# Five of eight slices of the split w1 and w2 are formed beside phase two's first pair, and stores move to GpSimd's queue

## The chip, the cores and the metric

The kernel runs on one core of one Trainium2 chip. The metric is the device time of one launch in microseconds (us). The time of a version is the median of several runs. A profiled execution also gives its span, from the first instruction to the last.

## The reference, cut to what matters

The inputs are float32 in the reference's code, and the ten arrays come to the kernel as 64-bit floats, which it reads as pairs of 32-bit words. Chunked attention (8 batches, 8 heads, 576 positions, chunks of 64) gives x of 4608 tokens by 512. Two gated products follow.

```
attn = softmax(scale * q_c @ k_c^T)          # in chunks of 64
x    = (attn @ v_c)  as [4608, 512]
x    = ((x @ w_a) * (x @ w_b)) @ w_out       # d_ff 1536: phase 0 below
out  = ((x @ w1) * (x @ w2)) @ w3 @ w_out2   # d_ff 1024: phase 1 below
```

## The kernel before, in words

The text calls the phase with d_ff 1536 phase one (`ph == 0` in the code) and the one with d_ff 1024 phase two (`ph == 1`). Tokens are worked in nine blocks of 512. Every matrix operand is split into a high and a low float32r part, and each product takes three passes (`SEQ`) of 128x512 matmuls.

Blocks are taken in pairs by a Strassen scheme of seven products (`strassen_step`) in place of eight. It works on slices of 128 columns of d_ff: twelve slices in phase one, eight in phase two. Its operands for each slice are the split pair of weights and two sums of them, four weight tiles. Block 0 and 1 go through plain products while weights are still being converted, pairs 1 to 3 of phase one through the scheme, and block 8 alone (the lone stage) through plain products again. Phase two has four pairs and block 8 alone.

The second product of a pair's first block follows slice by slice (`Second.part`). That of its second block comes afterwards in one stretch, which the code calls a burst. Its operands gh and gl are made by `ready` on ScalarE and GpSimd. After the last slice each 128x512 accumulator is copied out (`ev`, L845) and stored (L848) to a scratch in DRAM (`x2d`, 36 stores) or to the output (36 stores). Both kinds were issued by ScalarE's queue.

Weights are converted from 64-bit by `Conv`, driven by `Pump`. `float32_job` converts one piece of w3, w_out2, w1 or w2 and stores it as float32 in DRAM (40 stores, ScalarE's queue). A conversion's load goes to a slot of SBUF that an earlier conversion's store must have left.

In the lone stage `between` builds phase two's operands, while block 8 goes through twelve plain steps: 16 conversions of w1 and w2, w3 turned on TensorE (`turn_w3`), w3 @ w_out2 fused (`fuse`), and for each of the eight slices `Sums`: load the float32 pair, form two sums (`add`), split own parts (`own`) and sums (`early`), store all four tiles. These pieces are to be spent over 45 of the stage's 60 points, which is nine of its twelve steps.

A `Track` spreads pieces over points of a step. At one point it emits at most one piece that needs TensorE. SyncE's queue issues nearly all loads, in program order. Loads of q, k and v are put on a list (`ask`). `tick(loads=n)` issues n of them, and `settle` issues all that a unit needs at once. In phase one's pairs each of the seven products of a step ticks with 2 and each of the four parts of the second product with 1.

Of the kernel before, what the change touches and what calls it, by code (L numbers as in the profile page):

```python
# [18 lines left out]
NT = 512  # L19
# [59 lines left out]
def chunk_attention_two_gated_products(  # L79
# [55 lines left out]
    def store(to, src, wait=2, queue=None):  # L135

        stores.append([2 - wait, queue or nc.scalar, to, src])
# [490 lines left out]
    def w_tile(n, name):  # L628
        return pool.tile([P, 2, 2, 2, P], F32R, tag=f"w{n}", name=name)
# [4 lines left out]
    def by_part(t, s):  # L634

        return t[:, :, s].rearrange("p o k n -> p o (k n)")
# [32 lines left out]
    def float32_job(conv, to):  # L669


        def sink(w):
            store(to, w, 5)
            return (lambda: None), (lambda: None)

        return (conv, sink, nc.gpsimd)
# [48 lines left out]
    class Sums:  # L725
# [29 lines left out]
            split(by_part(t, 0), by_part(t, 1), v2, nc.vector)  # L755
            store(dw[self.ph][self.f][2 + i], whole(t).bitcast(F32), 2, nc.gpsimd)

        def own(self, m):


            o = slice(m, 2)
            t = w_tile(2 + m, f"w{self.ph}_{self.f}_o{m}")
            v2 = self.w[:, m].rearrange("p (o n) -> p o n", o=2)
            split(by_part(t, 0)[:, o], by_part(t, 1)[:, o], v2[:, o], nc.vector)
            store(dw[self.ph][self.f][m][:, m * NT :], whole(t)[:, m * NT :].bitcast(F32))

        def early(self, i):
            t = w_tile(6 + i, f"w{self.ph}_{self.f}_s{i}")
# [31 lines left out]
                n += 1  # L800

    def product(ps, w, x, begins):
        tick(loads=2)
        n = 0
        for wp, xp in SEQ:
            for kt in range(2):
                nc.tensor.matmul(  # L807
                    ps,
                    w[:, wp, kt],
                    x[:, kt, xp],  # L810
                    start=(begins and n == 0),
                    stop=(n == 5),
                    skip_group_check=True,
                )
                n += 1

    class Second:
# [6 lines left out]
        def part(self):  # L824
            m, ph, f, w, g = self.m, self.ph, self.f, self.w, self.g
            if m == 4:
                return
            self.m += 1
            tick(loads=1)
            acc = self.sums  # L830
            if f == 0:
                acc.append(psum.tile([P, NT], F32, tag=self.tags[m], name=f"acc{ph}_{self.j}_{m}"))
            ms = slice(m * P, (m + 1) * P)
            for wp, gp in SEQ:
                a, b = (w[:, wp, ms], g[gp]) if ph == 0 else (g[gp][:, ms], w[:, wp])
                nc.tensor.matmul(  # L836
                    acc[m],
                    a,
                    b,
                    start=(f == 0 and (wp, gp) == SEQ[0]),  # L840
                    stop=(f == NF[ph] - 1 and (wp, gp) == SEQ[-1]),
                )
            if f == NF[ph] - 1:
                t = pool.tile([P, NT], F32, tag="ev", name=f"ev{ph}_{self.j}_{m}", bufs=4)
                nc.scalar.copy(t, acc[m])  # L845
                j = self.j
                to = x2d[j][m] if ph == 0 else out[j * NT + m * P : j * NT + (m + 1) * P, :]
                nc.scalar.dma_start(to, t)  # L848

        def rest(self):  # L850
            while self.m < 4:
# [219 lines left out]
    with tc.manual_schedule():  # L1071
# [101 lines left out]
                pump.load(slot(6), nc.scalar)  # L1173
            tick(loads=8)
        units = unit_list(1)
        late = Track(attention_pieces(U[NHP:]), 5 * AHEAD)
        at = None
        for n, (T, f) in enumerate(order):
            if T == 0:
                conv = Track([conv_piece()] * (1 if f == 0 else 3), 5 if f + 1 < AHEAD else 8)  # L1180
                if f + 1 == NF[0]:
                    conv = None
            if T == 1 and f == 0:
                late.finish()
                attention_begins(units)
                at = Track(attention_pieces(units), 4 * (len(order) - n) - 2)

            def point(pe=True):
                if conv:
                    conv.point(pe)  # L1190
                (at or late).point(pe)

            if n + 1 == len(order):
                state["ready"] = ready(0, 1, 0, plain[0])
            plain_step(0, 0, T, f, f"0_{T}_{f}", point, plain[0], sums[0], "AC")
            if conv and (T == 1 or f + 1 < AHEAD):
                conv.finish()
                pump.flush()
# [11 lines left out]
        def summed(ph, f, n):  # L1210
            tag = dict(tag=f"Y{n % 3}")
            return Sums(ph, f, tag)

        def block_steps(ph, sb, x, at):

            single = sb == NSB
            j = LONE if single else 2 * sb
            nm = f"{ph}{sb}"
            new = ph == 0 and sb == 1
            sums, gplaces = [], None if single else []  # L1220
            n = NF[ph]
            su = first_sums
            last = single
            for f in range(n):
                extra = None
                if new:
                    if f + 2 < n:
                        su[f + 2] = summed(ph, f + 2, f + 2)
                        su[f + 2].load()
                    extra = Track(su[f + 1].pieces() if f + 1 < n else [], 5)  # L1230

                def freed(i):
                    if f + 2 < n:
                        if not new or i in (0, 3):
                            load_part(ph, f + 2, i)
                    elif ph == 0 and sb + 1 == NSB:
                        if i < 2:
                            load_plain(ph, f + 2 - n, i)
                    elif not last:
                        load_part(ph, f + 2 - n, i)  # L1240

                def point(pe=True):
                    if extra:
                        extra.point()
                    for a in at:
                        a.point(pe)

                if f + 1 == n and not single:
                    state["ready"] = ready(ph, j + 1, 0, gplaces)
                wo = state["outs"].next()  # L1250
                strassen_step(ph, j, f, x, f"{nm}_{f}", point, gplaces, sums, wo, freed)
                if extra:
                    extra.finish()
            for a in at:
                a.finish()
            return j, gplaces
# [20 lines left out]
        def between(got):  # L1277


            w3s, sums = [], []  # L1280
            turns = [(i, c) for i in range(NF[1]) for c in range(2)]
            for n_, ic in enumerate(turns + [None] * 2):
                if n_ >= 2 and n_ % 2 == 0:
                    w3s.append((1.5, True, lambda i=n_ // 2 - 1: fuse(i)))
                if ic:
                    w3s.append((1.0, True, lambda ic=ic: turn_w3(*ic)))
            su = [Sums(1, f, dict(tag=f"xo{3 + f % 2}")) for f in range(NF[1])]
            sums += [(0.1, False, su[0].load), (0.1, False, su[1].load)]
            for f in range(NF[1]):
                sums += su[f].early_pieces()  # L1290
                if f + 2 < NF[1]:
                    sums.append((0.1, False, su[f + 2].load))
            pump.cap = len(pump.jobs)
            pump.load(slot("L"))
            pump.load(slot("L"))
            conv = later_conv(2 * NF[1], "L")
            return merged((0, 1, w3s), (0, 0.75, conv), (0.3, 1, sums), (0, 0.5, x2_pieces([0, 1], got)))

        PTS = 7
        first_sums = {}  # L1300
# [3 lines left out]
        for ph, sb in [(0, sb) for sb in range(1, NSB + 1)] + [(1, sb) for sb in range(NSB + 1)]:  # L1304
# [5 lines left out]
            if lone:  # L1310
                x, pieces = lone_pieces(x32, f"{ph}{sb}")
                pieces = pieces + o2_pieces()
            elif not begins:
                x, pieces = strassen_pieces(x32, f"{ph}{sb}", sb == NSB)
            if ph == 0 and sb == 1:
                for f in range(2):
                    first_sums[f] = summed(ph, f, f)
                    first_sums[f].load()
                for f in range(2):
                    for i in (0, 3):  # L1320
                        load_part(ph, f, i)
                pieces = pieces + first_sums[0].pieces()
            steps, at, conv = NF[ph], [], []
            if ph == 0 and not lone:
                units = unit_list(sb + 1)
                attention_begins(units)
                work = attention_pieces(units)
                n_pts = PTS * steps + steps - 4
                if sb == NSB - 1:
                    pump.cap += 3 * NF[1]  # L1330
                    pump.load(slot(3))
                    pump.load(slot(3))
                    conv = later_conv(3 * NF[1], 3)
                    work = merged((0, 1, work), (0, 1, conv))
                    n_pts = PTS * steps
                at.append(Track(work, n_pts - 3))
# [92 lines left out]
```

## Time and profile before

| | |
|---|---|
| median of 3 runs | 1714.83 us (1713.59 to 1719.84) |
| the profiled execution | 1716.43 us, of which its span is 1714.6 us |
| TensorE (PE) busy | 1583.5 us, 92% of the span |
| VectorE (DVE), ScalarE (ACT), GpSimd (POOL) busy | 897.8, 552.3, 506.8 us |
| mean granted TensorE clock | 0.973 of full speed |
| moved by DMA | 409.56 MB, a mean of 239 GB/s |

The span is read by stages, since the engines and the queues have different limits in each. Block 0 and 1 take the time up to about 323 us with their burst. The pairs of phase one run to 955 us, with bursts at about 504, 710 and 922 us. The lone stage runs from 955 to 1145 us, and phase two fills the rest. Its first pair's steps run from 1145 to 1245 us.

### The profile page before, as it was taken

Reading aid. Unit: us, or ns where it says so; the run is one execution under the profiler, and the core shown is the slowest. Engines: PE = TensorE matmul, PEld = TensorE weight load, DVE = VectorE, ACT = ScalarE, POOL = GpSimd, SP = SyncE. Lnnn points to the kernel's source line nnn. Section 1 sums busy time; section 2 is a strip of 40 time slices with the busy share of each in tenths; the row PEclk is TensorE's granted clock in tenths of the full one; section 3 lists DMA queues with packets and bytes.
Section 4 is the critical chain, followed back from the end, with each engine's and each line's share of the span. In section 5 each row is a group of like instructions: output and inputs, shape, how many; then the busy total and the mean of one; then the engine's idle time right before and its main releaser. Section 6 shows DMA issues by size and latency. Waiting matters only on the chain.

```text
span 1714.6 us, 24613 instructions
## 1 busy us (share of the span) xinstructions
PE 1583.5 (92%) x8968; PEld 1265.1 (74%) x8968; DVE 897.8 (52%) x1460; ACT 552.3 (32%) x989; POOL 506.8 (30%) x450
## 2 busy tenths in 40 slices
PE   4779998899998999898999788899999999999998
PEld 3558786677776877676777676688878878878787
DVE  5767773766756555646786266552252252342331
ACT  4434443322243222322324223332141241242232
POOL 1434552222233111423335122212231232232322
PEclk9889999999999999999999899899999999999999
DMA  8667775877867887788987799987676676665684
GB/s 217 215 189 224 259 237 174 229 231 226 251 214 210 215 227 208 203 254 270 300 310 249 241 325 370 343 312 230 216 227 219 211 236 215 212 226 196 222 277 164
DMA packets 300536, 409.56 MB, mean 239 GB/s; under 512 B 176000, under 2 KB 196480, under 8 KB 300416
## 3 DMA queue, kind: packets, MB, share of 16 engines
q1 hardware_dynamic: 265568, 318.85, 61.4%
q0 software_dynamic: 12864, 46.14, 6.9%
q10 hardware_dynamic: 21984, 43.00, 6.7%
q8 instruction: 71, 1.16, 0.3%
q14 instruction: 49, 0.40, 0.1%
HBM read 321.91 MB, written 85.98 MB: 238 GB/s over the span
## 4 chain that ended last, share of the span: by engine, by line
PE 61%; DMA 13%; issue 8%; DVE 8%; POOL 4%; ACT 3%; SPq 2%; ACTq 0%; POOLq 0%; DVEq 0%
PE P L807 36%; PE acc L836 18%; SPq L148 2%; DMA wo<-dwo 2%; DMA d<-cv 2%; DMA cv<-in_moe_w_dram 2%; PE wf L1060 2%; PE pa L793 1%; DMA qk<-in_q_dram 1%; DVE c L895 1%; DMA cv_w<-in_moe_w_dram 1%; DMA dw<-w_o 1%; PE x L396 1%; PE pb L793 1%; DMA su<-d 1%
## 5 line engine op out<-in xcount | busy, mean ns | idle before, releaser
L807 PE MATMUL P<-xP,w 128*128 128x512 f32 (+1 forms) x3192 | 739.7, 385 | 25.0 <-DVE c L895 17.8
L807 PEld LDWEIGHTS P<-xP,w 128*128 128x128 f32 x3192 | 576.5, 189 | 157.9 <-DVE c L895 25.2
L895 DVE TENSOR_TENSOR c<-P,c 128x512 f32<-128x512 f32 (+1 forms) x228 | 150.0, 661 | 342.6 <-PE P L807 333.9
L923 POOL TENSOR_TENSOR G<-c,c 128x512 f32<-128x512 f32 x68 | 88.8, 1306 | 382.5 <-DVE c L895 382.3
L892 ACT COPY c<-P 128x512 f32<-128x512 f32 (+1 forms) x228 | 128.5, 564 | 223.3 <-PE P L807 219.7
L242 ACT CAST gh<-c 128x512 fp32r<-128x512 f32 x68 | 42.2, 621 | 356.6 <-DVE c L922 351.1
L243 POOL TENSOR_TENSOR gl<-c,gh 128x512 fp32r<-128x512 f32 x68 | 90.5, 1330 | 179.9 <-ACT gh L242 177.7
L836 PE MATMUL acc<-gh,wo 128*128 128x512 f32 x384 | 141.1, 405 | 0.0
L922 DVE TENSOR_TENSOR c<-P,c 128x512 f32<-128x512 f32 x68 | 46.9, 690 | 135.5 <-PE P L807 135.4
L836 PE MATMUL acc<-wo,gh 128*128 128x512 f32 x320 | 111.3, 391 | 0.5 <-ACT gh L242 0.5
L836 PEld LDWEIGHTS acc<-gh,wo 128*128 128x128 f32 x384 | 73.7, 192 | 16.8
L195 POOL TENSOR_TENSOR cv<-cv 128x512 f32<-128x512 f32 x40 | 46.8, 1170 | 107.7 <-DVE cv L189 76.4
L793 PE MATMUL pa<-xq,w 128*128 128x512 f32 x288 | 77.4, 421 | 0.0
L836 PE MATMUL acc<-gl,wo 128*128 128x512 f32 x192 | 76.5, 399 | 0.0
L793 PE MATMUL pb<-xq,w 128*128 128x512 f32 x288 | 71.9, 400 | 0.0
L845 ACT COPY ev<-acc 128x512 f32<-128x512 f32 x72 | 42.3, 588 | 88.8 <-PE acc L836 79.0
L836 PEld LDWEIGHTS acc<-wo,gh 128*128 128x128 f32 x320 | 60.1, 188 | 14.0 <-ACT gh L242 1.0
L243 DVE TENSOR_TENSOR xP<-xP,xP 128x512 fp32r<-128x512 f32 (+1 forms) x56 | 48.4, 905 | 40.5 <-ACT xP L242 40.5
L793 PEld LDWEIGHTS pa<-xq,w 128*128 128x128 f32 x288 | 57.5, 204 | 13.3
L836 PE MATMUL acc<-wo,gl 128*128 128x512 f32 x160 | 63.1, 394 | 0.8 <-POOL gl L243 0.8
L793 PEld LDWEIGHTS pb<-xq,w 128*128 128x128 f32 x288 | 54.5, 192 | 11.5
L1060 PE MATMUL wf<-wo,w3t 128*128 128x512 f32 x192 | 51.6, 429 | 11.6 <-DVE w3t L243 11.6
(153 smaller groups left out, 2358.8 us busy)
## 6 DMA issues: line engine op xcount, KB each, us to landing
w<-dw SPq DMA_DIRECT2D x228, 512.0 KB, 4.5
wo<-dwo SPq DMA_DIRECT2D x168, 512.0 KB, 4.6
dw<-w POOLq DMA_DIRECT2D x48, 512.0 KB, 5.1
w<-dw SPq DMA_DIRECT2D x92, 256.0 KB, 3.4
su<-d SPq DMA_DIRECT2D x20, 512.0 KB, 5.8
cv_o<-in_moe_w_out_dram SPq DMA_DIRECT2D x18, 512.0 KB, 5.4
x2d<-ev ACTq DMA_DIRECT2D x36, 256.0 KB, 4.8
x<-x2d SPq DMA_DIRECT2D x36, 256.0 KB, 4.7
```

The lines of the kernel that those rows point to most:

```text
L195: eng.tensor_tensor(self.w, hi.bitcast(F32), lo, op=ALU.add)
L242: nc.scalar.copy(dst_h, src)
L243: eng_l.tensor_tensor(dst_l, src, dst_h, op=ALU.subtract)
L793: nc.tensor.matmul(ps, w[m][:, kk // 2, wp, kk % 2], xq[kk // 2][:, kk % 2, xp], start=(n == 0), stop=(n == 3 * KM - 1),)
L807: nc.tensor.matmul(ps, w[:, wp, kt], x[:, kt, xp], start=(begins and n == 0), stop=(n == 5), skip_group_check=True,)
L836: nc.tensor.matmul(acc[m], a, b, start=(f == 0 and (wp, gp) == SEQ[0]), stop=(f == NF[ph] - 1 and (wp, gp) == SEQ[-1]),)
L845: nc.scalar.copy(t, acc[m])
L892: nc.scalar.copy(t, src)
L895: add = lambda o, a, b: nc.vector.tensor_tensor(o, a, b, op=ALU.add)
L922: nc.vector.tensor_tensor(g, last, c11, op=ALU.mult)
L923: nc.gpsimd.tensor_tensor(g_place(ph, nm.split("_")[0], f, gplaces), c22, c12, op=ALU.mult)
L1060: nc.tensor.matmul(ps, t[:, gp, jj], wo2[jj // 2][:, jj % 2, wp], start=(jj == 0 and (wp, gp) == SEQ[0]), stop=(jj == NF[1] - 1 and (wp, g ...
```

## The change

It does six things.

- `float32_job` gives its 40 stores to GpSimd's queue in place of ScalarE's, and `Second.part` its 72 stores.
- `own` puts its columns at the front of its tile and stores by GpSimd's queue too.
- In `between` only slices 0 to 2 are summed and split. Slices 3 to 7 are loaded as float32 in phase two's first pair, and `all_pieces` makes their four tiles there one step ahead of use; the tiles are used in place and also stored for the later pairs. The first pair loads no finished tiles for these slices.
- The conversions of w1 and w2 are spread over the whole of `between` and no longer over its first three quarters, the sums over its second half. The first two loads of these conversions are issued in the burst ahead of the stage.
- The attention pieces of block 1 and of pair 1 are one list, cut later, so that the first units of pair 1 are loaded and the first is turned while block 1's last unit is in work. Ahead of pair 1's burst q and k of the first unit of pair 2 are issued before one weight load.
- `product` ticks with 3 in place of 2.

```diff
@@ float32_job
-            store(to, w, 5)
+            store(to, w, 5, nc.gpsimd)
@@ class Sums
-        def own(self, m):
-            o = slice(m, 2)
-            t = w_tile(2 + m, f"w{self.ph}_{self.f}_o{m}")
-            v2 = self.w[:, m].rearrange("p (o n) -> p o n", o=2)
-            split(by_part(t, 0)[:, o], by_part(t, 1)[:, o], v2[:, o], nc.vector)
-            store(dw[self.ph][self.f][m][:, m * NT :], whole(t)[:, m * NT :].bitcast(F32))
+        def own(self, m, place=None):
+            t = w_tile(2 + m if place is None else place, f"w{self.ph}_{self.f}_o{m}")
+            v2 = self.w[:, m].rearrange("p (o n) -> p o n", o=2)[:, m:]
+            at = slice(0, 2 - m)
+            split(by_part(t, 0)[:, at], by_part(t, 1)[:, at], v2, nc.vector)
+            store(
+                dw[self.ph][self.f][m][:, m * NT :],
+                whole(t)[:, : (2 - m) * NT].bitcast(F32),
+                2,
+                nc.gpsimd,
+            )
+            return t
+
+        def all_pieces(self):
+            mine = pairs.setdefault((self.ph, self.f), {})
+
+            def own(m):
+                i = 3 * m
+                mine[i] = self.own(m, 4 * (self.f % 2) + i)
+
+            return [
+                (0.7, False, lambda: own(0)),
+                (1.7, False, self.add),
+                (0.7, False, lambda: self.part(0)),
+                (0.7, False, lambda: self.part(1)),
+                (0.4, False, lambda: own(1)),
+            ]
@@ product
-        tick(loads=2)
+        tick(loads=3)
@@ Second.part
-                nc.scalar.dma_start(to, t)
+                nc.gpsimd.dma_start(to, t)
@@ block 0 and 1
-        late = Track(attention_pieces(U[NHP:]), 5 * AHEAD)
+        both = attention_pieces(U[NHP:] + units)
+        cut = 1 + 8 * NHP
+        late = Track(both[:cut], 5 * AHEAD)
...
-                attention_begins(units)
-                at = Track(attention_pieces(units), 4 * (len(order) - n) - 2)
+                at = Track(both[cut:], 4 * (len(order) - n) - 2)
@@ block_steps
+        READY = 3
...
+            whole_new = ph == 1 and sb == 0
...
+                if whole_new:
+                    if READY <= f + 2 < n:
+                        su[f + 2] = Sums(ph, f + 2, dict(tag=f"Y{f % 2}"))
+                        su[f + 2].load()
+                    if READY <= f + 1 < n:
+                        extra = Track(su[f + 1].all_pieces(), 6)
...
                     if f + 2 < n:
+                        if whole_new and f + 2 >= READY:
+                            return
@@ between
-            su = [Sums(1, f, dict(tag=f"xo{3 + f % 2}")) for f in range(NF[1])]
+            su = [Sums(1, f, dict(tag=f"xo{3 + f % 2}")) for f in range(READY)]
...
-            pump.cap = len(pump.jobs)
-            pump.load(slot("L"))
-            pump.load(slot("L"))
             conv = later_conv(2 * NF[1], "L")
-            return merged((0, 1, w3s), (0, 0.75, conv), (0.3, 1, sums), (0, 0.5, x2_pieces([0, 1], got)))
+            return merged((0, 1, w3s), (0, 1, conv), (0.5, 1, sums), (0, 0.5, x2_pieces([0, 1], got)))
@@ ahead of the stages
+                pump.cap = len(pump.jobs)
+                slots["n"] = -1
+                pieces += [(0.1, False, lambda: pump.load(slot("L")))] * 2
...
-                for f in range(2):
-                    for i in (0, 3):
-                        load_part(ph, f, i)
+                for f, i in ((0, 0), (0, 3), (1, 0)):
+                    load_part(ph, f, i)
...
+                if sb == 1:
+                    settle(units[0].qk_end)
+                    load_part(ph, 1, 3)
```

## Rows read from the trace of the kernel before

**Rows 1.** The page, part 1: busy time of each engine.

```profile
PE 1583.5 (92%) x8968; PEld 1265.1 (74%) x8968; DVE 897.8 (52%) x1460; ACT 552.3 (32%) x989; POOL 506.8 (30%) x450
```

**Rows 2.** Busy time by stage: window, its length, each engine, clock, DMA.

```profile
284.00:323.00 39.00, 33.13 (x159) 25.63 (x158) 29.16 (x40) 16.06 (x30) 16.13 (x12) 0.91 0.75 209
...
955.00:1120.00 165.00, 135.75 (x569) 106.28 (x569) 91.00 (x158) 49.03 (x90) 36.67 (x39) 0.91 0.92 331
...
1145.00:1245.00 100.00, 100.00 (x436) 81.38 (x435) 24.93 (x37) 22.42 (x39) 21.25 (x17) 1.00 0.71 233
```

**Rows 3.** TensorE's timeline, lone stage: start, duration, group, wait before it.

```profile
967.52 1.11 PE L1050 MATMUL w3p<-ident,w 128*128 128x128 f32 x4 [6.06 <-DVE w3t L243]
971.55 8.08 PE L1060 MATMUL wf<-wo,w3t 128*128 128x512 f32 x24 [2.92 <-DVE w3t L243]
...
1054.76 7.50 PE L1060 MATMUL wf<-wo,w3t 128*128 128x512 f32 x24 [5.77 <-DVE w3t L243]
...
1095.54 1.11 PE L1050 MATMUL w3p<-ident,w 128*128 128x128 f32 x4 [3.83 <-DVE w3t L243]
...
1100.57 5.72 PE L1060 MATMUL wf<-wo,w3t 128*128 128x512 f32 x24
```

**Rows 4.** DMA issues from 955 to 1120 us: count, size, median us to landing.

```profile
dw<-w_s POOLq DMA_DIRECT2D x14, 512.0 KB, 8.2
d<-cv ACTq DMA_DIRECT2D x16, 256.0 KB, 6.2
...
su<-d SPq DMA_DIRECT2D x8, 512.0 KB, 7.5
...
dw<-w_o ACTq DMA_DIRECT2D x7, 512.0 KB, 7.4
```

**Rows 5.** Waits from 955 to 1120 us: total, times, longest.

```profile
SPq L173 <- DMA d<-cv: 54.9, 11, 9.3
```

**Rows 6.** DMA issues from 1145 to 1245 us, phase two's first pair.

```profile
w<-dw SPq DMA_DIRECT2D x24, 512.0 KB, 3.9
```

**Rows 7.** Groups by line: splits of the lone stage, evictions of the first pair.

```profile
L243 DVE TENSOR_TENSOR w_s<-su,w_s 128x512 fp32r<-128x512 f32 x14 | 12.9, 932 | 8.3 <-ACT w_s L242 8.3
...
L242 ACT CAST w_s<-su 128x512 fp32r<-128x512 f32 x14 | 8.6, 620 | 5.4 <-DMA dw<-w_s 4.2 <-DVE cv L185 1.2
...
L895 DVE TENSOR_TENSOR c<-P,c 128x512 f32<-128x512 f32 x24 | 16.6, 692 | 52.9 <-PE P L807 52.9
```

**Rows 8.** TensorE's timeline at block 1's seam.

```profile
124.66 1.09 PE L467 MATMUL t<-ident,qk 128*128 128x128 f32 x4 [5.66 <-DMA qk<-in_k_dram]
...
128.11 3.79 PE L793 MATMUL pa<-xq,w 128*128 128x512 f32 x12
```

**Rows 9.** Waits of SyncE's queue from 50 to 165 us.

```profile
SPq L173 <- DMA d<-cv: 54.5, 9, 16.7
```

**Rows 10.** TensorE's timeline in the first burst.

```profile
290.89 0.80 PE L836 MATMUL acc<-gh_1b,wo 128*128 128x512 f32 x1 [3.62 <-ACT gh_1b L242]
292.24 0.80 PE L836 MATMUL acc<-gl_1b,wo 128*128 128x512 f32 x1 [0.56 <-POOL gl_1b L243]
```

**Rows 11.** Waits of SyncE's queue from 280 to 345 us.

```profile
SPq L148 <- DMA x2d<-ev: 10.2, 2, 6.2
```

**Rows 12.** Waits of TensorE in later bursts, from 705 and from 1360 us.

```profile
PE acc L836 <- DMA wo<-dwo: 4.8, 4, 2.7
...
PE acc L836 <- POOL gl_3b L243: 1.0, 2, 0.8
```

**Rows 13.** Waits of SyncE's queue over the whole span.

```profile
SPq L713 <- PE P L807: 329.1, 160, 6.5
```

**Rows 14.** GpSimd's timeline at 60 us: three stores issued one after another.

```profile
59.99 0.57 POOL L157 DMA_DIRECT2D dw<-w  x1
...
61.09 0.54 POOL L157 DMA_DIRECT2D dwo<-wo  x1
```

**Rows 15.** ScalarE's timeline at the end: the last store's issue.

```profile
1711.48 0.34 ACTq L848 DMA_DIRECT2D out_dram<-ev  x1
```

More of the change, by code (lines that the diff above doesn't have):

```diff
@@ L1286, in between @@
                     w3s.append((1.0, True, lambda ic=ic: turn_w3(*ic)))
-            su = [Sums(1, f, dict(tag=f"xo{3 + f % 2}")) for f in range(NF[1])]
+            su = [Sums(1, f, dict(tag=f"xo{3 + f % 2}")) for f in range(READY)]
             sums += [(0.1, False, su[0].load), (0.1, False, su[1].load)]
-            for f in range(NF[1]):
+            for f in range(READY):
                 sums += su[f].early_pieces()
-                if f + 2 < NF[1]:
+                if f + 2 < READY:
                     sums.append((0.1, False, su[f + 2].load))
-            pump.cap = len(pump.jobs)
-            pump.load(slot("L"))
-            pump.load(slot("L"))
             conv = later_conv(2 * NF[1], "L")
-            return merged((0, 1, w3s), (0, 0.75, conv), (0.3, 1, sums), (0, 0.5, x2_pieces([0, 1], got)))
+            return merged((0, 1, w3s), (0, 1, conv), (0.5, 1, sums), (0, 0.5, x2_pieces([0, 1], got)))
         PTS = 7
```

## The prediction, made before the changed kernel ran

> **What bounds the kernel now.** I read the page's busy times first. TensorE is busy for 1583.5 of the 1714.6 us [rows 1], so about 131 us of the span are idle, and a change can win only where those lie, or where the granted clock is low. I then read the busy times by stage. In phase two's first pair TensorE is busy for the whole 100 us at full clock [rows 2]: nothing that is only moved there shows unless it makes TensorE wait. The large loss is in the lone stage's first nine steps. TensorE is busy for 135.75 of 165 us there, at a mean clock of 0.91, while the 16 DMA engines are busy for 0.92 of the time at 331 GB/s [rows 2].
>
> How much could come back there at most? Nine steps hold 9 x 36 = 324 matmuls and the eight fusions 8 x 24 = 192. A fusion at full clock takes 5.72 us for 24, or 0.238 each [rows 3], so 516 take 123 us. A turn of w3 takes 1.11 us at the slow clock [rows 3], so about 0.6 at full clock by an estimate, and sixteen add 10. So the floor is about 133 us, and 32 of the 165 us are lost.
>
> TensorE's timeline shows where. It names VectorE's `w3t` as releaser of every long wait, 6.06, 5.77 and 3.83 us [rows 3], but that split takes under 1 us by itself. It stands in VectorE's queue behind conversions that wait for their loads. Those stand on SyncE's queue, which waited 54.9 us in eleven goes for conversions' stores `d<-cv` to leave a slot [rows 5]. And each transfer takes 6.2 to 8.2 us to land in this stage [rows 4], against 3.9 us for a weight load in phase two's first pair [rows 6]. The chain is store, slot, load, conversion, VectorE, TensorE, and full DMA engines stretch it. After a long wait TensorE runs slowly too: the fusion behind the first takes 8.08 us and the one behind the second 7.50 against 5.72 [rows 3], as in a stretch granted 1.2 instead of 2.4 GHz for part of it.
>
> Two smaller losses were read in the timeline and in the queue's waits: the seam of block 1 [rows 8, 9] and the first burst [rows 10, 11].
>
> **The change part by part.** *Lone stage.* For each of five slices it removes a load of 512 KB, two stores of 512 KB and the own parts' stores of 512 and 256 KB (the first four in [rows 4], the last in the code), 2304 KB or 2.36 MB. That is 11.8 MB of 331 x 165 = 54.6 MB. Two loads of conversions (1.05 MB) go ahead of the stage. What is left, 41.8 MB, would need 126 us at the same 331 GB/s, less than TensorE's floor of 133: DMA engines stop being full for all of it, though sums and conversions still meet in the second half.
>
> The first stall, 6.06 us and 8.08 - 5.72 = 2.36 us of slow running, came from the first conversion's load. It is now issued a burst earlier, so I take it whole: 8.4 us. The second and third, 5.77 + (7.50 - 5.72) + 3.83 = 11.4 us, hang on the chain above, which gets shorter and doesn't vanish: I take 0.6 of it, 6.8 us. Of the idle time that remains, 29.25 - 6.06 - 5.77 - 3.83 = 13.6 us in short waits, most is TensorE waiting for its own turn to be split, since a fusion follows close on it; I take 2 us. Sum 17 us. The bounds are 8 (the first stall alone) and 32 (all of the loss). Conversions now end with the stage's ninth step, and the last store must leave its slot before phase two's operands are written there. A store takes 6.2 us to land [rows 4], and its issue is delayed by five ticks; three steps lie behind, so I cost it at nothing; without that cover it is one landing, 6 us.
>
> *Phase two's first pair.* Five steps each get 3.5 splits and four half-width adds. A split is 0.62 us on ScalarE and 0.93 on VectorE [rows 7]; an add of half the width is taken as no longer than one, so VectorE gets at most 3.5 x 0.93 + 4 x 0.93 = 7.0 us and ScalarE 2.2 us a step. A step lasts 12.5 us (100 by 8), in which VectorE is busy for 3.1 [rows 2] and its adds wait 52.9 us in all for TensorE [rows 7]. It fits. What hides it is that idle time; without the cover each split in front of an eviction would cost TensorE up to 0.9 us, some 3 us a step or 16 in all. Loads and stores are equal in number within 512 KB a step. I take 1 us, between 0 and 16, near the low end because the splits fall where the next eviction still waits for its product.
>
> *Seam of block 1.* TensorE waits 5.66 us for k of pair 1's first unit, and the twelve matmuls behind take 3.79 us [rows 8] where twelve at 0.238 take 2.9. SyncE stood for 16.7 us on one slot just before [rows 9], with that k behind it. In the new order this k is asked for ahead of the stand. I take 6 of these 6.6 us; the bounds are 0 (another unit's load gets stuck in its place) and 9 (the slow parts around it too).
>
> *First burst.* TensorE waits 3.62 + 0.56 us for gh and gl [rows 10], and the clock of the 39 us is 0.91 [rows 2]. A share of 0.18 at half speed gives 0.91; 0.18 x 39 = 7 us at half speed lose 3.5. Ahead of it loads of q and k stood on SyncE's queue until a store `x2d<-ev` had landed, 10.2 us in two waits [rows 11]; they read nothing that it writes. ScalarE's queue issues that store. With these stores on GpSimd's queue and q and k ahead of the weight load, I expect this to go: 4.2 + 3.5 = 7.7, of which I take 5.5, and 3 us for the second of the two waits (up to 6.2) that delays the next pair's sums. Bounds 2 and 14.
>
> *Later bursts.* Waits for wo, 4.8 us in the third [rows 12], lie behind the same loads; I take 3 us for the second and third burst together. Each later burst waits about 1.0 us for gl [rows 12], which ScalarE's four store issues of 0.34 us [rows 15] hold up. GpSimd now issues them at 0.55 us [rows 14] ahead of the third gl; the gh copy runs meanwhile. I take 4 us over six bursts, between a loss of 6 x 1.1 = 7 (two issues exposed) and a gain of 6.
>
> *Attention asked sooner.* A step's ticks ask for 7 x 3 + 4 = 25 loads in place of 18. I take 1 us of gain, between 5 and -5. *End.* The last store's issue takes 0.55 instead of 0.34 us [rows 14, 15], and a landing by that queue isn't shown; I take 1 us, between 0.2 and 2.
>
> *Sum.* 17 + 6 + 5.5 + 3 + 3 + 4 + 1 - 1 - 1 = 37.5 us off. The profiled execution took 1716.4 us (a span of 1714.6 and 1.8 around it), 1.6 more than the median. 1716.4 - 37.5 = 1679, and I forecast 1680 us for the median, between the two bases.
>
> *A rule against it.* The row shows SyncE's loads held for 10.2 us behind stores of another queue [rows 11], so I price moving these stores at a gain. The Trainium skill, DMA: Bandwidth & Descriptors, section Issuing engines are not separate DMA queues, says that the same 16 DMA engines serve all queues, and that spreading issues saves only issuing time. By the row the sum is 37.5 off, by the rule it is the second rival's.
>
> **The rivals.** *The queue still sets the lone stage's pace.* Conversions need store, slot and load in turn whatever else is moved. Stores of 6.2 us [rows 4] and as many waits [rows 5] speak for it, the 11.8 MB less against it. Only the first stall goes: 8.4 in place of 17, so 1680 + 9 = 1689 us.
>
> *Moving stores wins nothing.* If loads are late for other reasons than the stores ahead of them, the first burst, its following wait and the later bursts keep their time (5.5 + 3 + 3 + 4 = 15.5), and 1680 + 15.5 gives 1696 us. With the first rival too, 1705. For it speaks that many small loads stand ahead of wo; against it, the wait of 6.2 us for a store [rows 11].
>
> *It does not do what it says.* Work saved in the lone stage comes back as waits of TensorE in the first pair, 16 us, and the seams keep theirs: 1716.4 - 17 + 16, about 1715 us. Against it stands VectorE's idle time there [rows 7].
>
> *Slower: SyncE's queue chokes on attention loads.* 25 instead of 18 in each of 36 steps put seven more issues ahead of the weight loads. If these come late, TensorE waits at every step; 37.5 us by 36 steps is 1.0 us a step to cancel the gain, and from 1.3 on it is slower by over 0.5%. At 2 us a step: 1680 + 72 = 1752 us. Against it speaks that this queue waits 329.1 us for TensorE to leave weight tiles [rows 13], so it is ahead of its work; and the number of loads stays the same.
>
> **How the numbers follow.** My forecast has a chance of 0.5, the pace of conversions 0.15, no gain from moved stores (alone or with it) 0.17, no change 0.1, slower 0.08. 0.5% of 1714.8 is 8.6 us, about what a measurement of this kernel can tell from no change. Below 1706 lie the first three: faster 0.82. Within it 0.10, slower 0.08. The range reaches from 1658 (the upper gains in the lone stage, and in the first burst a part) to 1709, past the third case with both rivals; the last two stay outside.
>
> **What would show it.** Between the end of the fourth burst and phase two's first step about 173 us in place of 190, no wait of 6 us at its start, SyncE's waits for `d<-cv` under 40 us there, and landings near 5 us. The first pair still at 100 us with TensorE full. No wait for k at block 1's seam, none over 1 us at the first burst's second slice, and no SyncE wait for `x2d<-ev`. I would be wrong if TensorE's long waits in the lone stage stay with fewer bytes, if waits for VectorE appear in the first pair, or if GpSimd's store issues hold gl.

## The result and the profile after

The changed kernel takes 1668.66 us (median of 4, 1666.18 to 1671.03) against 1715.57 of the kernel before beside it. The ratio is 0.9723, with a 95% interval from 0.9698 to 0.9748: faster by 47 us, where 35 were forecast. The profiled execution took 1666.18 us, its span 1664.4. The same kernel was run again at the end, as the twelfth run, on another occasion: 1662.68 us and a ratio of 0.9677 (0.9657 to 0.9698). The median of the kernel before went from 1712.7 to 1724.65 us over the four occasions. So totals of runs made together are compared, and for the rest the stages of the profiles.

The page's busy times of the changed kernel, part 1, answer to [rows 1]:

```profile
PE 1570.5 (94%) x8968; PEld 1256.9 (76%) x8968; DVE 899.0 (54%) x1460; ACT 551.0 (33%) x989; POOL 571.5 (34%) x578
```

TensorE is idle for 93.9 us of the span where it was for 131.1. GpSimd has 128 instructions more, the moved stores, and is busy for 65 us more, 0.5 each. ScalarE's busy time is the same, since the time of issuing is counted for GpSimd and not for ScalarE.

The next table is worked out from the timelines: each stage ends where ScalarE starts to copy out the fourth accumulator of a block (L845 before, L867 after), so no missing matmul record enters. The last row runs to the span's end. The column "again" is the twelfth run. The row of the lone block is called the lone stage from here on; it reaches from the last eviction of the fourth burst into phase two, and so is longer than the 190 us of that stage's steps.

```
stage, up to the last eviction of    before   after   again
block 0                               285.7   281.8   279.0
first burst                            40.3    36.2    36.2
pair 1                                181.2   174.1   174.0
second burst                           36.6    35.8    34.9
pair 2                                169.0   168.9   168.9
third burst                            37.6    38.1    37.2
pair 3                                174.6   173.3   173.9
fourth burst                           31.4    32.4    31.5
lone block, into phase two            201.4   172.8   172.0
phase two, first pair                  93.6    92.6    92.6
phase two, four bursts together        83.6    79.1    79.1
phase two, pairs 2 to 4 together      310.1   309.9   309.9
last block                             65.6    64.6    64.8
to the span's end                       3.8     4.9     4.9
```

More than half of the 50 us of span come from the lone stage (28.6), then from pair 1 (7.1), the first burst (4.1), the start (3.9) and phase two's bursts (4.5). Busy time by stage in the changed kernel, for the first burst, the lone stage's first nine steps and the first pair's steps, with the columns of [rows 2]:

```profile
275.00:311.00 36.00, 32.54 (x191) 25.95 (x192) 27.64 (x36) 18.36 (x35) 16.64 (x16) 0.95 0.79 218
940.00:1076.00 136.00, 129.14 (x574) 102.64 (x573) 69.57 (x119) 40.56 (x72) 45.45 (x55) 0.97 0.88 314
1100.00:1200.00 100.00, 100.00 (x436) 81.25 (x435) 42.75 (x77) 33.02 (x61) 35.35 (x41) 1.00 0.72 260
```

The nine steps take 136 us in place of 165. TensorE waits for 7 of them and no longer for 29, at a mean clock of 0.97. The DMA engines are nearly as full as before, 0.88 against 0.92, and move 42.7 MB (314 x 136) in place of 54.6. The first pair hides all that came to it: VectorE goes from 24.9 to 42.8 us of the 100, and TensorE is still full. TensorE's longest waits in the lone stage, in its timeline:

```profile
948.90 0.83 PE L1072 MATMUL w3p<-ident,w 128*128 128x128 f32 x4 [2.40 <-DVE w3t L243]
951.30 8.00 PE L1082 MATMUL wf<-wo,w3t 128*128 128x512 f32 x24 [1.57 <-DVE w3t L243]
968.23 5.82 PE L1082 MATMUL wf<-wo,w3t 128*128 128x512 f32 x24 [0.41 <-DVE w3t L243]
```

The wait of 6.06 us of [rows 3] is 2.40, and those of 5.77 and 3.83 have no successor over 1.5. The first fusion still runs slowly, 8.00 us. DMA issues and waits from 940 to 1076 us answer to [rows 4, 5]:

```profile
d<-cv POOLq DMA_DIRECT2D x15, 256.0 KB, 5.1
...
dw<-w_s POOLq DMA_DIRECT2D x5, 512.0 KB, 5.2
...
su<-d SPq DMA_DIRECT2D x3, 512.0 KB, 6.3
```

```profile
SPq L173 <- DMA d<-cv: 43.4, 7, 7.7
```

Landings of the transfers of [rows 4] take 5.1 to 6.3 us in place of 6.2 to 8.2, but SyncE still stands for 43.4 us on conversions' slots. At block 1's seam, TensorE's timeline has the first unit of pair 1 earlier and, from 112 to 150 us, no wait over 1.1 us. SyncE's stands on conversions' slots, which the second fence shows for 50 to 165 us, add up to nearly as much as before, 50.0 us for 54.5 [rows 8, 9]:

```profile
113.33 1.04 PE L467 MATMUL t<-ident,qk 128*128 128x128 f32 x8
...
123.64 0.63 PE L480 MATMUL f<-ident,e 128*128 128x128 f32 x4 [1.10 <-DVE e L370]
```

```profile
SPq L173 <- DMA d<-cv: 50.0, 12, 10.8
```

In the first burst one wait of 0.51 us for wo is what TensorE's timeline shows in the place of [rows 10], and SyncE's waits from 270 to 335 us name no `x2d<-ev`, which was first there in [rows 11]:

```profile
290.70 0.47 PE L858 MATMUL acc<-gh_1b,wo 128*128 128x512 f32 x1 [0.51 <-DMA wo<-dwo]
```

```profile
SPq L148 <- PE x L396: 4.6, 1, 4.6
SPq L148 <- DMA wo<-dwo: 3.0, 4, 1.4
```

What made gh late in [rows 10] stands in ScalarE's timeline of the kernel before. The copy of the fourth accumulator ended there at 286.33 us, but its store was issued only at 289.85, and gh stood behind that store in program order:

```profile
285.74 0.59 ACT L845 COPY ev<-acc 128x512 f32<-128x512 f32 x1 [0.61 <-ACT ev L845]
289.85 0.33 ACTq L848 DMA_DIRECT2D x2d<-ev  x1
290.22 1.14 ACT L242 CAST gh_1b<-G0p 128x512 fp32r<-128x512 f32 x2 [3.89 <-DMA x2d<-ev]
```

So TensorE's 3.62 us came from a store that was held on ScalarE's own queue. In the changed kernel that queue has no stores of evictions.

### The profile page after: what moved, and what is told of

The parts are those of the page before. It is cut to its first block, busy times and chain, and to the rows that moved or that the text cites. A ratio compares the mean times of both kernels' runs of the same rounds, so it can differ in the third digit from the quotient of the medians.

```text
span 1664.4 us, 24572 instructions
## 1 busy us (share of the span) xinstructions
PE 1570.5 (94%) x8968; PEld 1256.9 (76%) x8968; DVE 899.0 (54%) x1460; ACT 551.0 (33%) x989; POOL 571.5 (34%) x578
## 4 chain that ended last, share of the span: by engine, by line
PE 73%; DVE 8%; DMA 5%; issue 4%; SPq 3%; ACT 3%; POOL 3%; POOLq 0%; DVEq 0%; ACTq 0%
PE P L829 39%; PE acc L858 20%; PE wf L1082 3%; PE pb L815 3%; PE pa L815 3%; SPq L148 3%; DMA wo<-dwo 2%; PE pa0L L815 2%; PE pb0L L815 1%; PE x L396 1%; DVE c L917 1%; PE s L345 1%; ACT xP L242 1%; DMA d<-cv 1%; POOL cv L195 1%
## 5 line engine op out<-in xcount | busy, mean ns | idle before, releaser
L829 PE MATMUL P<-xP,w 128*128 128x512 f32 (+1 forms) x3102 | 715.5, 383 | 20.2 <-DVE c L917 16.5
L829 PEld LDWEIGHTS P<-xP,w 128*128 128x128 f32 x3102 | 557.0, 188 | 148.0 <-DVE c L917 23.3
L243 DVE TENSOR_TENSOR xP<-xP,xP 128x512 fp32r<-128x512 f32 (+1 forms) x56 | 63.9, 1182 | 25.9 <-ACT xP L242 25.9
L867 ACT COPY ev<-acc 128x512 f32<-128x512 f32 x72 | 42.3, 587 | 71.0 <-PE acc L858 65.9
L157 POOL DMA_DIRECT2D dw<-w x58 | 32.4, 559 | 83.2 <-DVE w L243 80.3
```

The lines of the kernel that those rows point to most:

```text
L243: eng_l.tensor_tensor(dst_l, src, dst_h, op=ALU.subtract)
L829: nc.tensor.matmul(ps, w[:, wp, kt], x[:, kt, xp], start=(begins and n == 0), stop=(n == 5), skip_group_check=True,)
```

## The experiments

My theory was the forecast's: fewer bytes and an earlier first load shorten the lone stage, stores on another queue free SyncE's loads in the first burst and behind it. The rivals were that the stores' queue did it all, that it did nothing, and, later, that the new spread of pieces did it. Runs 1 to 4, 5 to 8 and 9 to 12 were made together.

**Runs 1 to 4: bytes, queues, first loads.** Run 1 keeps all eight slices in the lone stage. That needs the old spread too, as sums may not come ahead of their conversions.

```diff
-        READY = 3
+        READY = 8
-            return merged((0, 1, w3s), (0, 1, conv), (0.5, 1, sums), ...
+            return merged((0, 1, w3s), (0, 0.75, conv), (0.3, 1, sums), ...
```

> The changed kernel with all eight slices summed and split in the lone stage again (READY 8, and the old spread of conversions and sums, which eight slices need); everything else as changed. By fewer bytes as the cause, the stage from the fourth burst to the lone block's evictions goes from 172.8 us back by about 17 and the time is about 1686 us. If instead the stores' queue made that stage shorter, it stays within 4 us of 172.8 and the time near 1670 us.

Measured: 1684.80 us, lone stage 193.4 us, 20.6 more than the changed kernel's 172.8. The queue alone is out as the cause. Run 2 takes the moved stores back, run 3 moves them in the kernel before.

```diff
-            store(to, w, 5, nc.gpsimd)
+            store(to, w, 5)
...
-                nc.gpsimd,
+                nc.scalar,
...
-                nc.gpsimd.dma_start(to, t)
+                nc.scalar.dma_start(to, t)
```

> The changed kernel with the 40 float32 stores, the own parts' stores and the 72 stores of evictions on ScalarE's queue again. By my theory the first burst and pair 1 lose about 8 us and the lone stage 3 at most: about 1680 us. By the rule that queues share the DMA engines nothing is lost: 1669 us. If the queue is what shortened the lone stage, that stage is 10 us or more longer: 1690 us.

> The kernel before with the same three kinds of stores on GpSimd's queue and nothing else. By my theory the first burst, pair 1 and the later bursts gain some 11 us: 1704 us. By the rule, 1715 us. If the queue shortens the lone stage too, 1690 us.

Measured: 1677.44 us for run 2 and 1698.96 for run 3 (ratio 0.9914, 0.9882 to 0.9945). By stages, with the changed kernel between them:

```
stage              before   run 3 (moved alone)   after   run 2 (moved back)
first burst          40.3          36.3            36.2         36.9
pair 1              181.2         176.0           174.1        182.1
pair 2              169.0         168.8           168.9        172.7
pair 3              174.6         174.7           173.3        176.8
lone stage          201.4         196.2           172.8        171.9
phase two, bursts    83.6          79.1            79.1         83.5
```

Pair 1's gain is the queue's: taken back, 8.0 us return. By all fourteen profiles the gain is 6.7 us: the two with stores of evictions on ScalarE's queue have 181.2 and 182.1 us, the twelve with them on GpSimd's 174.0 to 176.4, with a mean of 175.0. The first burst gets faster by the queue alone or by the order of loads alone. Phase two's bursts gain 4.5 us by the queue. The lone stage gains 5 by it while it is crowded, and nothing when it isn't, by one profile each. SyncE's waits in run 2 from 270 to 340 us begin with the old ones:

```profile
SPq L148 <- DMA x2d<-ev: 7.9, 3, 3.8
SPq L148 <- DMA wo<-dwo: 3.7, 6, 1.0
```

Loads of q, k and v again stand behind stores that they have nothing to do with. The traces record by which semaphore each DMA reports its landing, and this shows how. In all fourteen profiles the DMAs of SyncE and ScalarE share eight semaphores, and those of GpSimd have eight others. In the kernel before, none of 1512 DMAs is issued before the one that used its semaphore last has landed, so that at most eight of SyncE's and ScalarE's are under way. In this way a store that is slow to land holds up a later DMA on either queue. The fourth store above has the semaphore of the first, which landed at 289.77 us. The next load of k on SyncE's queue, issued at 290.61, has that of the second store, which landed at 290.60. Issues of SyncE within 0.2 us of such a landing of ScalarE's number 23 in the kernel before, 14 in run 2, and one each in runs 1 and 12. No run changed the semaphores, so this is read from the traces and not tested by itself.

How a late load reaches TensorE is seen in pair 1 of the kernel before. VectorE waits 5.96 us for k, the eviction of a product stands behind that in its program order, and TensorE waits 3.13 us for the eviction:

```profile
370.24 0.71 DVE L334 STREAM_TRANSPOSE kT<-qk 128x512 f32<-128x512 f32 x1 [5.96 <-DMA qk<-in_k_dram]
371.59 8.79 PE L807 MATMUL P<-xP,w 128*128 128x512 f32 x30 [3.13 <-DVE c L922]
```

Run 2 has the same pair of waits with 4.64 and 4.77 us at 429.02 and 430.96 us. In the changed kernel VectorE waits in pair 1 for no k for 1 us or more.

The Trainium skill, DMA: Bandwidth & Descriptors, section Issuing engines are not separate DMA queues, says that issuing from several engines saves only the time of issuing. ScalarE issues four of these stores at the head of pair 1, at 0.33 us each, and their move is worth 6.7 us there: in this program more was saved than the time of issuing.

Pairs 2 and 3 are 3.7 to 3.9 and 2.1 to 3.5 us longer in run 2 than in the other three kernels of the table, and no run explains it. Pair 2 can take longer by itself: run 5, with the stores on GpSimd's queue, has 171.8 us there, and the twelve profiles beside these two have 168.8 to 169.0.

Run 4 issues the first two loads of w1 and w2 at the stage's start.

```diff
-                pump.cap = len(pump.jobs)
-                slots["n"] = -1
-                pieces += [(0.1, False, lambda: pump.load(slot("L")))] * 2
+            pump.cap = len(pump.jobs)          # in between()
+            slots["n"] = -1
+            pump.load(slot("L"))
+            pump.load(slot("L"))
```

> The changed kernel with the first two loads of w1 and w2 issued at the start of the lone stage again. By my theory the first stall of 6 us and its slow clock come back there: 8 us, 1677 us. If the first stall was only the crowd of transfers at the stage's start, which is smaller now, 1670 us.

Measured: 1666.44 us, lone stage 176.5, so 3.7 us and not 8. The wait came back nearly whole, 5.71 us in TensorE's timeline, but the slow fusion behind it is there with and without:

```profile
947.17 1.12 PE L1072 MATMUL w3p<-ident,w 128*128 128x128 f32 x4 [5.71 <-DVE w3t L243]
949.69 8.22 PE L1082 MATMUL wf<-wo,w3t 128*128 128x512 f32 x24 [1.40 <-DVE w3t L243]
```

**Run 5: the seam as two lists.** The edit puts back the two lists and `attention_begins` at block 1's first step.

```diff
-        both = attention_pieces(U[NHP:] + units)
-        cut = 1 + 8 * NHP
-        late = Track(both[:cut], 5 * AHEAD)
+        late = Track(attention_pieces(U[NHP:]), 5 * AHEAD)
...
+                attention_begins(units)
-                at = Track(both[cut:], 4 * (len(order) - n) - 2)
+                at = Track(attention_pieces(units), 4 * (len(order) - n) - 2)
```

> The changed kernel with the attention of block 1 and of pair 1 as two lists again, the second begun at block 1's first step. By my theory the wait for k of 5.7 us and its slow clock come back: some 6 us more up to block 0's evictions, which is 284 to 286 us there against 278 to 282 in the runs with one list, and about 1673 us. If that stretch only scatters from run to run, it stays within 277 to 282 us.

Measured: 1669.57 us, 284.3 us up to block 0's evictions. The wait for k is back in TensorE's timeline:

```profile
124.59 1.08 PE L467 MATMUL t<-ident,qk 128*128 128x128 f32 x4 [5.89 <-DMA qk<-in_k_dram]
```

The three profiles with two lists have 285.7, 284.2 and 284.3 there, the eleven with one list 274.4 to 281.8 with a mean of 278.1. So the one list is worth 6.6 us, by stages; the stretch scatters by 7 us, which is why one pair of profiles shows 3.9.

**Run 6: two loads a product.**

```diff
-        tick(loads=3)
+        tick(loads=2)
```

> The changed kernel with 2 loads asked for at each product in place of 3. By my theory pair 1 changes by 1 us or less, and the time is 1669 us: its gain of 7 us came with the stores' queue. If asking sooner made that gain, pair 1 goes from 174 back towards 181 us and the time to 1675.

Measured: 1661.08 us, pair 1 at 174.2, pair 2 at 168.8, pair 3 at 174.2 us. Asking for three is worth nothing beside the moved stores. The lower total lies up to block 0's evictions (276.2 us), where this edit changes nothing.

**Run 7: the old spread with three slices.**

```diff
-            return merged((0, 1, w3s), (0, 1, conv), (0.5, 1, sums), ...
+            return merged((0, 1, w3s), (0, 0.75, conv), (0.3, 1, sums), ...
```

> The changed kernel, with three slices in the lone stage still, but conversions over the first three quarters of its pieces and the sums from 0.3 on, as before. By my theory the bytes decide and the lone stage (172.8 us) gets 2 us longer at most. If the even spread made the gain, it gets 8 us or more longer, with waits for conversions' loads in its first half.

Measured: 1676.17 us, lone stage 186.8 us, 14.0 more, with the same bytes. My theory of bytes falls in its size. The busy times of run 7's first nine steps, a turn of w3 in TensorE's timeline, and the chain of work ahead of TensorE's wait of 3.19 us for that turn's split (start, duration, what):

```profile
937.00:1086.00 149.00, 132.97 (x568) 104.99 (x567) 71.88 (x118) 38.70 (x70) 45.44 (x55) 0.94 0.81 288
```

```profile
1006.53 0.60 PE L1072 MATMUL w3p<-ident,w 128*128 128x128 f32 x4
```

```profile
1007.32 0.68 DVE w_o L243
1008.00 1.19 DVE cv L179
1009.22 0.67 ACT cv L180
1009.88 0.55 ACT gh0L L242
1010.43 0.49 ACT w3t L242
...
1010.95 0.70 DVE w3t L243
...
1011.70 7.39 PE wf L1082 x24
```

The chain names no transfer. The turn had ended at 1007.13 us, and its split began on ScalarE at 1010.43, 3.3 us later, behind other pieces. Conversions, sums and the split of w3 stand in VectorE's and ScalarE's queues in program order, so `w3t` waits for what was emitted before it. Crowded into less of the stage, more stands before it. That the DMA engines are less full on the mean, 0.81 against 0.88, follows from the same bytes in a longer stretch. But neither were they fuller in the part into which run 7 crowds the conversions, the first three quarters, here of run 7 and of the changed kernel:

```profile
937.00:1049.00 112.00, 98.14 (x415) 77.61 (x414) 56.75 (x92) 28.76 (x52) 36.04 (x43) 0.93 0.86 300
940.00:1042.00 102.00, 95.36 (x422) 75.92 (x421) 48.78 (x83) 28.20 (x49) 32.19 (x39) 0.97 0.86 303
```

SyncE's stands on conversions' slots are 44.6 us against 43.4, and VectorE's waits for conversions' loads 3.9 us in three against none. So far as these rows show, VectorE's 3.9 us are the only part of the 14 us that hangs on transfers.

**Run 8: q and k ahead of two more bursts, last stores on ScalarE.**

```diff
-                if sb == 1:
-                    settle(units[0].qk_end)
+                settle(units[0].qk_end)
+                if sb == 1:
                     load_part(ph, 1, 3)
...
-                nc.gpsimd.dma_start(to, t)
+                (nc.scalar if ph == 1 and j == LONE else nc.gpsimd).dma_start(to, t)
```

> The changed kernel with two more edits: the last block's four output stores on ScalarE's queue again, and q and k of the next pair's first unit issued ahead of the second and third burst too, as ahead of the first. By my theory the end (4.9 us from the last eviction) goes back to 3.8, and TensorE's waits for wo in those two bursts, 3.0 and 4.5 us, fall under 2 each: 5 us in all, about 1664 us. If wo is late because the loads after these stand ahead of it, only the 1 us at the end is won.

Measured: 1671.22 us. The second burst goes to 40.5 us from 35.8 and the third to 40.0 from 38.1. TensorE's waits from 480 to 535 us and SyncE's timeline there:

```profile
PE acc L858 <- DMA wo<-dwo: 6.9, 3, 5.2
```

```profile
484.42 3.90 SPq L148 DMA_DIRECT2D qk<-in_q_dram  x8
488.37 4.31 SPq L148 DMA_DIRECT2D qk<-in_k_dram  x8
492.79 0.47 SPq L701 DMA_DIRECT2D wo<-dwo  x1
493.30 5.13 SPq L148 DMA_DIRECT2D v<-in_v_dram  x8
498.52 0.53 SPq L701 DMA_DIRECT2D wo<-dwo  x1
```

Sixteen small loads keep SyncE issuing for 8 us ahead of wo. The end got 0.8 us shorter (4.1), but the last block longer by 1.0.

**Runs 9 and 10: what in the spread.** Run 9 has the conversions spread evenly and only the sums early. Run 10 puts six slices into the lone stage, with the even spread.

```diff
@@ run 9
-            return merged((0, 1, w3s), (0, 1, conv), (0.5, 1, sums), ...
+            return merged((0, 1, w3s), (0, 1, conv), (0.3, 1, sums), ...
@@ run 10
-        READY = 3
+        READY = 6
-            return merged((0, 1, w3s), (0, 1, conv), (0.5, 1, sums), ...
+            return merged((0, 1, w3s), (0, 1, conv), (0.6, 1, sums), ...
```

> The changed kernel with the three slices' sums from 0.3 of the lone stage's pieces on, as before, and the conversions evenly over all of them, as changed. If the even spread of conversions made the 14 us between the seventh run's lone stage (186.8) and 172.8, this stays within 3 us of 172.8. If it was the later sums, it goes to about 185.

> Six slices summed and split in the lone stage in place of three (7.1 MB more), conversions evenly over all of it, sums from 0.6 on, which is as many slices as can come behind their conversions. If the even spread makes the gain and bytes count for little, the lone stage is 173 to 179 us. If the bytes decide as I forecast, 11.8 MB for 17 us, it is 183 or more.

Measured: 1666.14 us and a lone stage of 176.6 us for run 9; 1675.44 and 182.8 for run 10. Of the 14.0 us the conversions' spread makes 10.2 and the later sums 3.8. Three slices more cost 10.0 us at nearly the even spread, 3.3 a slice, which is at the edge of the second case. That is also the forecast's price, 17 us for five or 3.4 a slice; at the old spread five slices cost 6.6 us. A slice brings bytes and work for VectorE and ScalarE alike, and no run separates the two.

**Runs 11 and 12: a version that takes the useful edits, and the changed kernel.** Run 11 has the edit of run 6 and the second of run 8; run 12 is the changed kernel.

> The changed kernel with 2 loads asked for at each product and the last block's four stores on ScalarE's queue. From the stages of the sixth and eighth run: the end 1 us shorter and pairs as before, 2 to 6 us under the changed kernel timed beside it. If the sixth run's lower time was scatter of the first stretch, 1 us under it.

> The changed kernel as it is, for the comparison beside the eleventh run and for the scatter of the first stretch, up to block 0's evictions: 281.8 us in its first profile and 276 to 282 in five others with the same code there. I expect 276 to 282 and a time of 1662 to 1670 us.

Measured: 1662.68 us both (1661.40 to 1666.66 and 1660.65 to 1663.68). No version here beats the changed kernel beyond scatter.

## Why the prediction was right, and where its sum was off

The time lay in the range and on the forecast side. The sum said 37.5 us off; 47 were measured by the medians. Term by term:

*Lone stage, 17 us forecast, 28.6 measured: the term of the sum that was mis-sized.* From 201.4 us, run 1 reaches 193.4 with all but the moved slices and the spread (8.0 us); run 7 moves five slices at the old spread, 186.8 (6.6 us more); the spread makes the other 14.0, down to 172.8. I costed the spread at nothing. It was possible only because slices were moved: eight sums need their conversions early. So bytes and spread belong together, and run 10 shows 10.0 us for three slices when the spread stays. The step that failed is the chain that I read, behind the first stall, from waits for `d<-cv` and full DMA engines. In run 7 the transfers are no more crowded and the stage is longer, and what stands ahead of `w3t` is work on VectorE and ScalarE. That this order of queues makes the remaining waits is read from the chain; no run took the queue's order apart by itself. The trace before had a sign of it. Of VectorE's waits for conversions' loads in this stage, 25.7 us in four, 22.3 are the first stall, and the other three come to 3.4 us:

```profile
DVE cv L179 <- DMA cv<-in_moe_w_dram: 25.7, 4, 22.3
```

Nor did SyncE's waits for `d<-cv` fall under 40 us as forecast (43.4). Between the fourth burst and phase two's first step 160 us pass, where 173 were the sign. At the old spread the stage gains 14.6 us (run 7), close to the 17, but not by the chain that was named: that closeness is luck. TensorE's floor of 133 us for the nine steps held: the changed kernel takes 136, so 29 of the 32 us that I called lost came back, near my upper bound.

*First stall, 8.4 us of those 17.* Run 4 gives 3.7. The wait returned without the early load (5.71 for 2.40), as forecast, but the slow fusion did not go with it: 8.00 and 8.22 us.

*First pair, 1 us of cost forecast.* None: its steps are full, and VectorE's extra work is 17.8 us for five slices or 3.6 a step, half of my bound of 7.0.

*Seam, 6 us.* 6.6 by fourteen profiles, for the reason given: with two lists (run 5) the wait for k is back; SyncE's stands on slots remained (50.0 us), and the k that had been behind them came before.

*First burst 5.5 and the next pair 3.* 4.1 and 7.1 us, the second 6.7 by all profiles. In the burst the reading was wrong, though the size was near: gh was late by a store held on ScalarE's queue, and not by the loads that stood on SyncE's. Run 2 shows it: SyncE waits 7.9 us for `x2d<-ev` again, ScalarE's four stores go out 1.0 us apart, and the burst takes 36.9 us. In pair 1 the mechanism held, loads held up by `x2d<-ev`, and was sized too small: 3 us were costed, for one of two waits.

*Later bursts.* For wo in the second and third, 3 us were forecast and no clear gain came (36.6 and 37.6 before, 35.8 and 38.1 after, 34.9 and 37.2 again). Run 8 gives a reason: loads of attention ahead of wo delay it, and these still stand there when the stores are gone. The 4 us over six bursts came as 4.5 in phase two's four; the fourth burst gained nothing.

*Asking sooner, 1 us.* Nothing, by run 6. *End, 1 us of cost.* 1.1 us, as forecast.

The rival that the queue still sets the lone stage's pace is refuted by the stage, which gained 28.6 us and not 8.4, the rival that moved stores win nothing by runs 2 and 3. SyncE's queue did not choke: pairs 1 to 3 lost nothing at 25 loads a step.

## What to carry to other kernels

Work that must come behind other work limits how that other work may be spread; when some of it is moved elsewhere, spread the rest again, for the spread may be worth more than what was moved. A store that is slow to land can hold up loads that have nothing to do with it, and whatever stands behind the next store on its own engine: look in the queues' waits for the names of stores. Before the cause of a wait is called a transfer, run a version with the same transfers in another order.

## What the runs showed that I had not expected

With the same bytes, and DMA engines as full in its crowded part (0.86 in both), a stage was 14 us shorter by the order of its pieces. And a stretch whose code is the same in ten profiles took 274.4 to 281.8 us, while phase two's pairs agreed within 0.1 us; run 2, whose stores differ in that stretch, has 278.5.
